# Two more head pairs turned on TensorE, wider weight rows and a re-dealt order of loads and normalising in an attention and feed-forward kernel

## The chip, the cores and the metric

One Trainium2 chip, one of its cores. The metric is the device time of one execution in microseconds (us); lower is better. Three runs of the kernel before gave 489.35, 489.85 and 490.97 us, median 489.85.

## The reference

Attention over 8 batches of 12 heads (448 rows of 64), with one added to the softmax's denominator, then a feed-forward layer with the Mish function over the 3584 rows of 768:

```
scores = matmul(q, k.T) / sqrt(64);  m = max(scores, -1)
e = exp(scores - m)
attn = e / (sum(e, -1) + exp(-m) + 1e-9)
x = matmul(attn, v), heads side by side: [3584, 768]
h = x @ w_in                             # 768 x 2048
out = (h * tanh(softplus(h))) @ w_out    # 2048 x 768
```

Inputs and output are float32; the kernel computes in bfloat16 and sums in float32.

## The kernel before

**Pairs and steps.** Two heads make a pair, 48 pairs in all, numbered here from 0 (the fifth is pair 4, the twelfth pair 11, the sixteenth pair 15). A pair has 7 tiles of 128 query rows against 448 keys, dealt over four steps of 2, 2, 2 and 1 tiles (in the first batches the single tile is the last rows of one head with the first of the other). A step is: TensorE (PE) multiplies the scores into one of three score buffers in PSUM; VectorE (DVE) takes the negated row maximum (`tensor_reduce`, L270); ScalarE (ACT) takes the exponentials into `en` and their sums (L283). `scores_ahead` (L222) keeps the three buffers filled, so the scores of step i+3 come as soon as the exponentials of step i have freed a buffer.

**From exponentials to x.** `denominators` (L295) and `normalise` (L302) scale the 7 tiles of `en` by the reciprocal denominator (L317 on DVE; L315 on GpSimd, which is POOL, for the last pair of a unit). Then `en` is turned so that keys lie on partitions, in tile `eT`. There are two ways. A DMA transposition issued by SyncE (SP) at L321 turns a whole pair. `turn_on_pe` (L326) turns a quarter of a pair (index j) with 7 PE transposes (L332) into a PSUM tile, and a copy of 112x896 elements to `eT` (L336) is put on the list `late`. Pairs in `BY_PE` (5, 6 and 7) go the second way. `av_pair` (L344) multiplies `eT` by v, 8 matmuls at L358, and leaves a copy into `xT` (L367) on `late`. `flush_late` issues what stands on `late`.

**The two mo tiles.** PSUM has two tiles `mo0` and `mo1` outside the score buffers. `mo_take` (L107) hands out the one that was freed first. Turns, q and k transposes, `av_pair` in the first units, and the feed-forward matmuls all take from these two. The order on each engine is the order of the program text. So a PE instruction that takes a tile waits for the copy that last emptied it, and everything behind it on PE waits too.

**Stages.** The head runs the six pairs of batch 0 alone (L511 to L538). Then comes a loop over units u of three pairs (L540). A unit has 12 attention steps n (L551), which also work off a planned list of second matmuls (`mm2_part`, L417) spread by `weight`; then 8 blocks of first matmul and Mish (`mm1_mish`, L375), between which the three pairs are normalised and the next three pairs' q and k are transposed by PE (L179) and copied out. Unit 2 has no second matmuls and no spare work, unit 3 neither; unit 4 (`first_mm2`) is the first that has them, with 5 quarter blocks where later units have 7. Tables place the single acts by unit and step: `TURN_AT` (L491) the quarters turned on PE, `AV_AT` (L496) the av of pairs 3 to 8, `W_AT` (L498) the weight loads.

**Loads.** SP issues q, k and v of a pair, three DMAs of 224 KB (`load_pair`, L114), between its DMA transpositions, all in program order. POOL casts them to bfloat16 (`cast_pair`, L151; pair 0's q and k are cast by DVE and ACT), and issues the weight loads with a cast on the way (`load_w`, L145): 12 pieces of w_in, each [128, 2, 512], three pieces to a quarter of d_ff; and 8 of w_out. The head issues six pieces, units 2, 3 and 4 the rest.

Of the kernel before, what the change touches and what calls it, by code (L numbers as in the profile page):

```python
# [15 lines left out]
UNIT_PAIRS = 3  # L16
# [3 lines left out]
def kernel(  # L20
# [21 lines left out]
    UNITS_PER_B = HP // UNIT_PAIRS  # L42
# [3 lines left out]
    NH = d_model // 2  # L46
# [33 lines left out]
    w_in_sb = singles.tile([128, DM_T, d_ff], BF16)  # L80
# [18 lines left out]
    loaded, casted, qkT, att, xT, gT, o_sbs, stats = {}, {}, {}, {}, {}, {}, {}, {}  # L99
# [3 lines left out]
    def flush_late():  # L103
        while late:
            late.popleft()()
# [5 lines left out]
        return mo_free.popleft()  # L111


    def load_pair(p):  # L114
        if p >= N_PAIRS:
            return
        b, h0 = p // HP, (p % HP) * 2
        tiles = []
        for nm, src in (("q", q), ("k", k), ("v", v)):
            t = ld_pool.tile([SP_, 2, NT * D], FP32, tag=f"{nm}_f", name=f"{nm}_f")  # L120
            nc.sync.dma_start(
                out=t, in_=src[b, h0 : h0 + 2].rearrange("h (p t) d -> p h (t d)", t=NT)
            )
            tiles.append(t)
        loaded[p] = tiles


    def w_pieces():
        c_in, c_out = d_ff // 4, NH
        for i in range(4):  # L130
            for a in range(0, DM_T, 2):
                yield (
                    w_in_sb[:, a : a + 2, i * c_in : (i + 1) * c_in],
                    moe_w_in[a * 128 : (a + 2) * 128, i * c_in : (i + 1) * c_in],
                )
        for h in range(2):
            for f in range(0, FF_T, 4):
                yield (
                    w_out_sb[:, f : f + 4, h * c_out : (h + 1) * c_out],
                    moe_w_out[f * 128 : (f + 4) * 128, h * c_out : (h + 1) * c_out],  # L140
                )
# [6 lines left out]
            nc.gpsimd.dma_start(out=dst, in_=src.rearrange("(a p) c -> p a c", p=128))  # L148


    def cast_pair(p):  # L151
        if p >= N_PAIRS:
            return
        q_f, k_f, v_f = loaded.pop(p)
# [7 lines left out]
        cast_q(out=q_bf, in_=q_f.rearrange(by_t, t=NT))  # L162
        cast_k(out=k_bf, in_=k_f.rearrange(by_t, t=NT))  # L163
        nc.gpsimd.tensor_copy(out=v_bf, in_=v_f)  # L164
        casted[p] = (q_bf, k_bf, v_bf)

    def transpose_pair(p, bank=None):
        if p >= N_PAIRS:
# [53 lines left out]
    def scores_ahead(limit):  # L222

        while rg["next"] < limit and rg["used"] < len(sc_tiles):
            rg["used"] += 1
            scores(rg["next"])
            rg["next"] += 1
# [71 lines left out]
        )  # L299
        nc.vector.reciprocal(out=st["rden"], in_=st["den"])  # L300

    def normalise(p, dma=True, on_pool=False):  # L302
        st = att[p]
        en = st["en"]
        if on_pool:

            st["rden2"] = st_pool.tile([128, NTILE], FP32, tag="rden2", name="rden2")
            nc.vector.tensor_copy(out=st["rden2"], in_=st["rden"])  # L308
        for i in range(NTILE):
            args = dict(  # L310
                out=en[:, :, i, 0:SP_], in0=en[:, :, i, 0:SP_],
                scalar1=st["rden2" if on_pool else "rden"][:, i : i + 1],
            )
            if on_pool:
                nc.gpsimd.tensor_scalar(scalar2=1.0, op0=ALU.mult, op1=ALU.mult, **args)  # L315
            else:
                nc.vector.tensor_scalar(scalar2=None, op0=ALU.mult, **args)  # L317
        eT = eT_pool.tile([128, NT, 2 * S], BF16, tag="eT", name="eT")
        st["eT"] = eT
        if dma:  # L320
            nc.sync.dma_start_transpose(  # L321
                out=eT.rearrange("c j (i q) -> c (j i) q", q=128),
                in_=en.rearrange("q j i c -> q (j i c)"),
            )

    def turn_on_pe(p, j, act=False):  # L326

        st = att[p]
        own = mo_take()
        ps = own[:, :].bitcast(BF16).rearrange("c (i q) -> c i q", q=128)  # L330
        for i in range(NTILE):
            nc.tensor.transpose(ps[0:SP_, i, :], st["en"][:, j, i, 0:SP_], ident)  # L332
        copy = nc.scalar.copy if act else nc.vector.tensor_copy

        def evac():
            copy(  # L336
                out=st["eT"][0:SP_, j, :].rearrange("c (i q) -> c i q", q=128),
                in_=ps[0:SP_, 0:NTILE, :],
            )
            mo_free.append(own)  # L340

        late.append(evac)
# [116 lines left out]
    first_mm2 = 2 * UNITS_PER_B  # L459
# [7 lines left out]
    for g in range(B // 2):  # L467
# [12 lines left out]
        else:  # L480
# [17 lines left out]
    W_AT = ({5: 1, 9: 1}, {1: 1, 4: 1, 5: 1, 7: 1, 9: 1, 11: 1}, {3: 1, 5: 1, 7: 1, 9: 1})  # L498
    for p in range(UNIT_PAIRS):
        load_pair(p)  # L500
    for p in range(2):
        cast_pair(p)
# [36 lines left out]

    for u in range(UNITS_PER_B, N_UNITS + 2 * UNITS_PER_B):  # L540
        attn = u < N_UNITS
# [4 lines left out]
        p0 = u * UNIT_PAIRS  # L546
# [4 lines left out]
        for n in range(steps):  # L551
            pi, s = divmod(n, STEPS)
            p, idx = p0 + pi, p0 * STEPS + n
            late_tp = u == UNITS_PER_B and n == STEPS
            if late_tp:
                transpose_pair(p0 + 2)
            exps(idx)
            if late_tp:
                evac_qk(p0 + 2)
            if u == UNITS_PER_B + 1:  # L560
                for part in TURN_AT[1].get(n, []):
                    turn_on_pe(*part)
            flush_late()
            acc += weight[n]
            want = int(total * acc / sum(weight) + 1e-6)
            while done < want:
                fn, w = filler.popleft()
                fn()
                done += w
            scores_ahead(end)  # L570
            if n in LOAD_AT:
                load_pair(p0 + LOAD_AT.index(n) + LEAD)
                cast_pair(p0 + LOAD_AT.index(n) + LEAD - 1)
            if u - UNITS_PER_B < len(AV_AT):
                early = AV_AT[u - UNITS_PER_B]
                if n in early:
                    av_pair(early[n])
                if u == UNITS_PER_B:
                    for part in TURN_AT[0].get(n, []):
                        turn_on_pe(*part)  # L580
# [65 lines left out]
```

## Time and profile before

| | us |
|---|---|
| median of the runs | 489.85 |
| profiled execution, own time | 492.75 |
| its span | 491.0 |
| PE busy | 450.5 (92%) |
| DVE busy | 351.3 (72%) |
| ACT busy | 350.2 (71%) |
| POOL busy | 161.5 (33%) |

Stretches of the span, read from the timelines and from a table of windows:

| stretch, us | what | PE busy, us | DVE busy, us | ACT busy, us |
|---|---|---|---|---|
| 16 to 30 | head | 7.70 of 14.0 | 13.42 | 12.00 |
| 30 to 47 | head | 10.36 of 17.0 | 14.48 | 15.14 |
| 47 to 66 | end of head, unit 2 attention | 16.78 of 19.0 | 18.06 | 14.08 |
| 66 to 78 | unit 2 first matmul | 11.44 of 12.0 | 9.72 | 7.44 |
| 78 to 94 | unit 3 attention | 11.12 of 16.0 | 14.38 | 14.27 |
| 105.6 to 120.5 | unit 4 attention | 12.90 of 14.9 | 12.02 | 13.61 |
| 132.3 to 149 | unit 5 attention | 14.83 of 16.7 | 10.86 | 13.59 |
| 149 to 162 | unit 5 first matmul | 12.00 of 13.0 | 11.35 | 8.43 |
| 188.6 to 215.3 | a later unit | 26.69 of 26.7 | 21.23 | 21.95 |

How to read the lines that follow: a timeline line is start, duration, engine, source line, operation, what it writes and reads, how often; in brackets stands how long the engine had been idle before it and what ended that. PEld is a weight load on TensorE, SPq is SP's queue. In the strips each digit is a fortieth of the span in tenths busy.

### The profile page before, as it was taken

The page shows a single profiled execution, that of the slowest core. Times are in us where ns is not written, and L with a number is a line of the kernel's source. Part 1 is how long each engine was busy: PE and PEld are TensorE (multiplying, and loading weights), DVE is VectorE, ACT ScalarE, POOL GpSimd, SP SyncE. Part 2 cuts the span into 40 slices and gives each one's busy share as a digit, 9 for nine tenths or more (in the row PEclk, how much of TensorE's full clock was granted, in tenths as well). Part 3 has the DMA queues.
Part 4 walks back from the last instruction along what each step waited for, and adds up shares of the span by engine and source line. Part 5 has one row for each costly group of instructions (what it writes and reads, how often), then busy time and mean ns, then how long its engine had stood idle before and what let it go on. Part 6 is the DMA issues. An engine that isn't in the chain of part 4 may idle for free.

```text
span 491.0 us, 8804 instructions
## 1 busy us (share of the span) xinstructions
PE 450.5 (92%) x2992; PEld 248.5 (51%) x2992; DVE 351.3 (72%) x702; ACT 350.2 (71%) x906; POOL 161.5 (33%) x266
## 2 busy tenths in 40 slices
PE   3556898798989999999999999999999999999996
PEld 1222444454644555555655555555556565556563
DVE  4798987978868787878788786878797878420021
ACT  4889678878777887979796878888797979502300
POOL 3622257454412534253413323253425230300000
PEclk9999998999999999999999999999999999999999
DMA  8999999999999999999998979998999686780112
GB/s 212 183 205 228 236 207 221 228 177 236 175 225 263 195 220 188 241 186 267 148 248 187 223 164 210 211 213 227 176 265 179 167 176 140 132 159 21 45 37 93
DMA packets 209452, 92.19 MB, mean 188 GB/s; under 512 B 166272, under 2 KB 205952, under 8 KB 209408
## 3 DMA queue, kind: packets, MB, share of 16 engines
q1 hardware_dynamic: 201920, 85.35, 81.2%
q0 software_dynamic: 7488, 6.29, 8.8%
q8 instruction: 23, 0.38, 0.3%
q14 instruction: 21, 0.17, 0.1%
HBM read 45.61 MB, written 11.01 MB: 115 GB/s over the span
## 4 chain that ended last, share of the span: by engine, by line
PE 68%; DVE 14%; ACT 9%; DMA 4%; issue 2%; SPq 1%; POOL 0%; DVEq 0%; ACTq 0%
PE mo L446 24%; PE mo L382 23%; PE sc L249 8%; ACT en L283 8%; DVE negm L270 7%; PE sc L358 6%; DVE en L317 4%; PE sc L382 3%; PE sc L179 3%; DMA eT<-en 3%; DMA k_f<-in_k_dram 1%; PE mo L358 1%; PE sc L255 1%; DVE xT L367 1%; DVE eT L336 1%
## 5 line engine op out<-in xcount | busy, mean ns | idle before, releaser
L283 ACT ACTIVATE en<-sc,negm 128x448 bf16<-128x448 f32 x336 | 209.7, 637 | 28.7 <-DVE negm L270 16.3
L270 DVE TENSOR_REDUCE negm<-sc 128x2 f32<-128x896 f32 x192 | 182.4, 969 | 61.5 <-PE sc L249 48.7
L446 PE MATMUL mo<-w_out_sb,gT 128*128 128x384 bf16 (+1 forms) x896 | 142.1, 303 | 0.0
L382 PE MATMUL mo<-xT,w_in_sb 128*128 128x448 bf16 x672 | 140.2, 352 | 0.9 <-DVE xT L367 0.9
L388 ACT ACTIVATE gT<-mo 128x448 bf16<-128x448 f32 x112 | 59.4, 543 | 73.5 <-PE mo L382 73.3
L446 PEld LDWEIGHTS <-gT 128*128 128x128 bf16 x896 | 84.0, 98 | 46.8 <-issue 1.3
L382 PEld LDWEIGHTS <-w_in_sb 128*128 128x128 bf16 x768 | 72.8, 98 | 64.9 <-issue 4.2
L315 POOL TENSOR_SCALAR en<-en,rden 128x448 bf16<-128x448 bf16 x98 | 61.7, 649 | 115.8 <-DVE rden L308 106.0
L249 PE MATMUL sc<-kT,qd 128*128 128x448 bf16 x252 | 71.6, 354 | 1.8 <-DVE qd L210 1.5
L162 POOL CAST q_bf<-q_f 112x512 bf16<-112x512 f32 x47 | 29.1, 619 | 121.8 <-DMA q_f<-in_q_dram 105.4
L283 ACT ACTIVATION_READ_ACCUMULATOR en<-sc,negm 128x1 f32 x336 | 69.2, 206 | 0.0
L317 DVE TENSOR_SCALAR en<-en,rden 128x448 bf16<-128x448 bf16 x238 | 67.2, 354 | 0.9
L433 DVE COPY o_sb<-mo 128x384 f32<-128x384 f32 (+1 forms) x64 | 32.1, 502 | 41.3 <-PE mo L446 41.2
L249 PEld LDWEIGHTS <-qd 128*128 128x128 bf16 x252 | 24.0, 97 | 32.1 <-issue 13.9
L358 PE MATMUL sc<-eT,v_bf 112*64 112x448 bf16 x288 | 34.1, 357 | 4.1 <-ACT en L283 2.0
L164 POOL CAST v_bf<-v_f 112x512 bf16<-112x512 f32 x48 | 29.6, 618 | 20.6 <-DMA v_f<-in_v_dram 19.1
L358 PEld LDWEIGHTS <-v_bf 112*64 112x64 bf16 x384 | 21.1, 114 | 25.7 <-issue 16.9
L255 PE MATMUL sc<-kT,qd 64*128 64x448 bf16 x36 | 17.5, 508 | 17.4 <-ACT en L283 16.0
L163 POOL CAST k_bf<-k_f 112x512 bf16<-112x512 f32 x47 | 29.2, 622 | 6.7 <-DMA k_f<-in_k_dram 5.9
L210 DVE TENSOR_SCALAR qd<-sc 64x448 bf16<-64x448 bf16 x72 | 27.8, 386 | 0.9
L218 ACT COPY kT<-sc 128x448 bf16<-128x448 bf16 x39 | 20.8, 534 | 6.8 <-PE sc L179 6.8
L446 PE MATMUL mo<-w_out_sb,mid 128*128 128x384 bf16 x128 | 24.9, 326 | 0.0
(50 smaller groups left out, 306.9 us busy)
## 6 DMA issues: line engine op xcount, KB each, us to landing
q_f<-in_q_dram SPq DMA_DIRECT2D x48, 224.0 KB, 5.5
k_f<-in_k_dram SPq DMA_DIRECT2D x48, 224.0 KB, 5.6
v_f<-in_v_dram SPq DMA_DIRECT2D x48, 224.0 KB, 5.9
w_in_sb<-in_moe_w_in_dram POOLq DMA_DIRECT2D x12, 256.0 KB, 5.6
w_out_sb<-in_moe_w_out_dram POOLq DMA_DIRECT2D x8, 384.0 KB, 8.6
out_dram<-o_sb SPq DMA_DIRECT2D x7, 336.0 KB, 3.5
out_dram<-o_sb SPq DMA_DIRECT2D x8, 288.0 KB, 4.8
out_dram<-o_sb SPq DMA_DIRECT2D x8, 240.0 KB, 3.4
```

Source lines behind the costliest of these rows:

```text
L163: cast_k(out=k_bf, in_=k_f.rearrange(by_t, t=NT))
L164: nc.gpsimd.tensor_copy(out=v_bf, in_=v_f)
L249: nc.tensor.matmul(sc[:, bk, 0:S], lhsT=qT[:, i].rearrange("d h r -> d (h r)"), rhs=kT, start=True, stop=True,)
L270: nc.vector.tensor_reduce(out=negm, in_=sc[:, 0 : len(cols), 0:S], axis=AX.X, op=ALU.max, negate=True)
L283: nc.scalar.activation(out=st["en"][:, :, c, 0:SP_], in_=sc[:, bk, 0:S].rearrange("q (j c) -> q j c", j=NT), func=AF.Exp, bias=st["negm"][ ...
L315: nc.gpsimd.tensor_scalar(scalar2=1.0, op0=ALU.mult, op1=ALU.mult, **args)
L317: nc.vector.tensor_scalar(scalar2=None, op0=ALU.mult, **args)
L358: nc.tensor.matmul(av[h * 64 : (h + 1) * 64, 0:S], lhsT=v_bf[:, h, j * D : (j + 1) * D], rhs=e_h, start=(j == 0), stop=(j == NT - 1),)
L382: nc.tensor.matmul(h_ps[:, 0:S], lhsT=w_in_sb[:, dm, ff * 128 : (ff + 1) * 128], rhs=xT[b][:, dm, :], start=(dm == 0), stop=(dm == DM_T - 1),)
L388: nc.scalar.activation(out=gT[b][:, ff, :], in_=h_ps[:, 0:S], func=AF.Mish)
L433: nc.vector.tensor_copy(out=o_sb[:, cols], in_=st["o"][:, 0:n_cols])
L446: nc.tensor.matmul(st["o"][:, 0:n_cols], lhsT=src[:, ff, c0 : c0 + 128], rhs=w_out_sb[:, ff, cols], start=(ff == 0), stop=(ff == FF_T - 1),)
```

## The change

Five things. (1) `BY_PE` gains pairs 4 and 11, so these are turned by 4 times 7 PE transposes each and not by DMA; pair 4 in unit 2 at n = 0 to 3, with pair 5 moved from n = 1 to 4 to n = 4 to 7, and pair 11 in unit 4 at n = 2, 4, 5, 7. Two of pair 4's copies go to ACT. In units 2 and 4 a turn now comes before the step's scores, and in unit 2 the av of pairs 3 and 4 come a step later. (2) A w_in piece is [128, 1, 1024]: six pieces to a half of d_ff, 12 in all as before. (3) In the head the 7 tiles of `normalise` are dealt 2, 2, 3 over three steps and no longer all in the second; pair 5's come in unit 2's first three steps. (4) The first three pairs' q and k are loaded ahead of their v, and their v are cast after all q and k. (5) Pair 15 is loaded in unit 4 at n = 0 and no longer in unit 3 at n = 6.

```diff
-    def load_pair(p):
+    def load_pair(p, which="qkv"):
...
-        c_in, c_out = d_ff // 4, NH
-        for i in range(4):
-            for a in range(0, DM_T, 2):
+        c_in, c_out = d_ff // 2, NH
+        for i in range(2):
+            for a in range(DM_T):
                 yield (
-                    w_in_sb[:, a : a + 2, i * c_in : (i + 1) * c_in],
+                    w_in_sb[:, a : a + 1, i * c_in : (i + 1) * c_in],
...
-        for i in range(NTILE):
+        for i in tiles:
...
+        if tiles[-1] < NTILE - 1:
+            return
...
-    BY_PE = (HEAD - 1, HEAD, HEAD + 1)
+    BY_PE = (HEAD - 2, HEAD - 1, HEAD, HEAD + 1, 2 * HEAD - 1)
+    DEALT = ((0, 1), (2, 3), (4, 5, 6))
     TURN_AT = (
-        {1 + j: [(HEAD - 1, j)] for j in range(NT)},
+        {**{j: [(HEAD - 2, j)] for j in range(NT)}, **{4 + j: [(HEAD - 1, j)] for j in range(NT)}},
...
+        {n: [(2 * HEAD - 1, j)] for j, n in enumerate((2, 4, 5, 7))},
     )
-    AV_AT = ({5: 3, 7: 4, 10: 5}, {5: 6, 8: 7, 10: 8})
+    AV_AT = ({6: 3, 8: 4, 10: 5}, {5: 6, 8: 7, 10: 8})
-    for p in range(UNIT_PAIRS):
-        load_pair(p)
+    for which in ("qk", "v"):
+        for p in range(UNIT_PAIRS):
+            load_pair(p, which)
...
-    cast_pair(2)
+    cast_pair(2, with_v=False)
+    for p in range(UNIT_PAIRS):
+        cast_v(p)
...
-            if s == 1:
-                if p:
-                    normalise(p - 1)
+            if s < len(DEALT) and p:
+                normalise(p - 1, dma=p - 1 not in BY_PE, tiles=DEALT[s])
...
-    normalise(HEAD - 1, dma=HEAD - 1 not in BY_PE)
+
+    def turn_parts(u, n):
+        for p, j in TURN_AT[u - UNITS_PER_B].get(n, []):
+            turn_on_pe(p, j, act=p == HEAD - 2 and j % 2 == 1)
...
             flush_late()
+            if u == UNITS_PER_B:
+                turn_parts(u, n)
...
+            if u == first_mm2:
+                turn_parts(u, n)
             scores_ahead(end)
+            if u == UNITS_PER_B and n < len(DEALT):
+                normalise(HEAD - 1, dma=False, tiles=DEALT[n])
             if n in LOAD_AT:
-                load_pair(p0 + LOAD_AT.index(n) + LEAD)
-                cast_pair(p0 + LOAD_AT.index(n) + LEAD - 1)
+                i = LOAD_AT.index(n)
+                if u == first_mm2 and i == 0:
+                    load_pair(p0 + LEAD - 1)
+                if u != first_mm2 - 1 or i < 2:
+                    load_pair(p0 + i + LEAD)
+                cast_pair(p0 + i + LEAD - 1)
...
-                if u == UNITS_PER_B:
-                    for part in TURN_AT[0].get(n, []):
-                        turn_on_pe(*part)
```

More of the change, by code (lines that the diff above doesn't have):

```diff
@@ L117, in load_pair @@
         b, h0 = p // HP, (p % HP) * 2
-        tiles = []
+        tiles = loaded.setdefault(p, [])
         for nm, src in (("q", q), ("k", k), ("v", v)):
+            if nm not in which:
+                continue
             t = ld_pool.tile([SP_, 2, NT * D], FP32, tag=f"{nm}_f", name=f"{nm}_f")
@@ L124, in load_pair @@
             tiles.append(t)
-        loaded[p] = tiles
     def w_pieces():
-        c_in, c_out = d_ff // 4, NH
-        for i in range(4):
-            for a in range(0, DM_T, 2):
+        c_in, c_out = d_ff // 2, NH
+        for i in range(2):
+            for a in range(DM_T):
                 yield (
-                    w_in_sb[:, a : a + 2, i * c_in : (i + 1) * c_in],
-                    moe_w_in[a * 128 : (a + 2) * 128, i * c_in : (i + 1) * c_in],
+                    w_in_sb[:, a : a + 1, i * c_in : (i + 1) * c_in],
+                    moe_w_in[a * 128 : (a + 1) * 128, i * c_in : (i + 1) * c_in],
                 )
@@ L148, in load_w, with cast_v, cast_pair @@
             nc.gpsimd.dma_start(out=dst, in_=src.rearrange("(a p) c -> p a c", p=128))
-    def cast_pair(p):
+    def cast_v(p):
+        nc.gpsimd.tensor_copy(out=casted[p][2], in_=loaded.pop(p)[2])
+    def cast_pair(p, with_v=True):
         if p >= N_PAIRS:
             return
-        q_f, k_f, v_f = loaded.pop(p)
+        q_f, k_f = loaded[p][:2]
         q_bf = bf_pool.tile([SP_, NT, 2, D], BF16, tag="q_bf", name="q_bf")
@@ L163, in cast_pair @@
         cast_k(out=k_bf, in_=k_f.rearrange(by_t, t=NT))
-        nc.gpsimd.tensor_copy(out=v_bf, in_=v_f)
         casted[p] = (q_bf, k_bf, v_bf)
+        if with_v:
+            cast_v(p)
     def transpose_pair(p, bank=None):
@@ L300, in denominators, with normalise @@
         nc.vector.reciprocal(out=st["rden"], in_=st["den"])
-    def normalise(p, dma=True, on_pool=False):
+    def normalise(p, dma=True, on_pool=False, tiles=range(NTILE)):
         st = att[p]
@@ L507 @@
     load_pair(3)
-    cast_pair(2)
+    cast_pair(2, with_v=False)
+    for p in range(UNIT_PAIRS):
+        cast_v(p)
     for p in range(HEAD):
@@ L560 @@
             if u == UNITS_PER_B + 1:
-                for part in TURN_AT[1].get(n, []):
-                    turn_on_pe(*part)
+                turn_parts(u, n)
             flush_late()
+            if u == UNITS_PER_B:
+                turn_parts(u, n)
             acc += weight[n]
@@ L569 @@
                 done += w
+            if u == first_mm2:
+                turn_parts(u, n)
             scores_ahead(end)
+            if u == UNITS_PER_B and n < len(DEALT):
+                normalise(HEAD - 1, dma=False, tiles=DEALT[n])
             if n in LOAD_AT:
[L572 to L573 removed]
+                i = LOAD_AT.index(n)
[4 more added lines that the diff above has]
+                cast_pair(p0 + i + LEAD - 1)
             if u - UNITS_PER_B < len(AV_AT):
@@ L577 @@
                     av_pair(early[n])
-                if u == UNITS_PER_B:
-                    for part in TURN_AT[0].get(n, []):
-                        turn_on_pe(*part)
             elif s == (2 if pi else 0) and N_PAIRS <= p < N_PAIRS + UNIT_PAIRS:
```

2 lines of the change are left out of this document (1 added, 1 removed).

## The prediction

> **What bounds the kernel now.** I read the page's strips first, then the timelines of PE, DVE, POOL and SP's queue up to 165 us, then the chain that ended last.
>
> ```profile
> PE   3556898798989999999999999999999999999996
> DVE  4798987978868787878788786878797878420021
> ```
>
> From the fourteenth slice (160 us) on PE is full; a later unit has 26.69 us of PE work in 26.7. Nothing in the change touches those units, so all is decided before 162 us, by when PE work begins and by how much is added. Before that PE is idle for 40.5 us of the span (491.0 less 450.5), most of it in the head, where DVE sets the pace (13.42 busy of 14.0 in 16 to 30 us).
>
> ```profile
> 10.57 0.62 POOL L162 CAST q_bf<-q_f 112x512 bf16<-112x512 f32 x1 [0.36 <-DMA q_f<-in_q_dram]
> 11.55 0.62 POOL L163 CAST k_bf<-k_f 112x512 bf16<-112x512 f32 x1 [0.36 <-DMA k_f<-in_k_dram]
> 41.25 0.80 POOL L162 CAST q_bf<-q_f 112x512 bf16<-112x512 f32 x1 [5.64 <-PE sc L258]
> ```
>
> Casts of pairs 2 and 7. At the start loads land 0.97 us apart and each cast waits for its own. The third line is released, I think, by its load (issued at 35.44, next view), since the engine named was long done.
>
> ```profile
> 22.73 5.65 SPq L321 DMA_TRANSPOSE eT<-en  x1
> 28.48 0.53 SPq L121 DMA_DIRECT2D q_f<-in_q_dram  x1
> ...
> 30.10 5.25 SPq L321 DMA_TRANSPOSE eT<-en  x1
> 35.44 0.53 SPq L121 DMA_DIRECT2D q_f<-in_q_dram  x1
> ```
>
> SP is a second chain: a transposition holds its queue for over 5 us, and the loads of pairs 6 and 7 stand behind.
>
> ```profile
> 57.14 0.53 PE L179 MATMUL mo<-ident,q_bf 112*128 112x112 bf16 x4 [0.41 <-DVE eT L336]
> ...
> 58.82 0.91 PE L332 MATMUL mo<-ident,en 128*112 128x128 bf16 x7 [0.27 <-DVE kT L216]
> ```
>
> In unit 2, PE work that takes an mo tile waits for the DVE copy that empties it.
>
> ```profile
> 125.13 12.44 DMA eT<-en
> 137.57 0.04 issue
> 137.61 0.95 PE sc L358 x8
> ```
>
> In the chain, pair 12's transposition takes 12.44 us (median of the transpositions 7 to 8), while four w_out loads run, and PE idles 1.87 us before 137.61.
>
> **Part by part.**
>
> *q and k ahead of v.* Pair 1's q and k move up one slot (0.97 us), pair 2's two (1.95). By the row of casts, pair 2's k is cast at 9.6 and not 11.55. Pair 3 still lands at 13.49 to 14.5, so its transposes keep the gain of the steps to some 1.5 us. The v casts move behind; no av needs v before 35 us, so nothing is paid.
>
> *Normalising dealt.* DVE's work is the same. It fills the 0.25 us that DVE waits in each pair after the denominators, about 1 us over the head. But the DMA transposition now follows one reduce (1.0) later. For pair 0: 22.73 less 1.5, plus 1.0, less 0.25: about 22.0. So the SP chain gains 0.7. Pairs 6 and 7 are loaded behind it, and PE's transposes of pair 7 and the av behind them give the last scores of the head's fifth pair (44.79). DVE, ahead by 1.75 by then, waits there. I take 0.7 of gain at 47 us; the bounds are 0 (the SP chain unmoved) and 2.5 (1.5 and 1.0, SP not binding).
>
> *Pair 4 by PE.* Removed: one SP transposition (about 6 us of the queue, after 51 us), so the loads of pairs 9 to 11, issued at 57.31 to 65, start up to 6 us earlier. That matters in one place: pair 8's normalise at 67.87 took 3.34 us beside POOL's casts of these loads; alone 7 tiles took 1.80. PE's wait for the q that comes behind it (0.56 us at 71.56) goes: 0.56 gained. Added in unit 2: 28 transposes on PE, four times 0.95 us as 58.82 shows; two copies on DVE (0.55 each, 1.1); two on ACT, not in the trace in this shape: between 0.53 (a 448-wide copy) and 1.1 (two of them), I take 0.8; ACT has 4.9 us idle in 47 to 66 to hide them. DVE is full from 46 to 61.4, so 1.1 counts. Then the order: at n = 4 the chain is now pair 8's transposes, DVE's two copies, pair 5's first turn in the tile so freed, and only then the scores. DVE has no work for 1.0 us (turn 0.55 and scores 0.36 at the faster rows, 0.95 and 0.55 at the slower: 1.5). At the end pair 4's and 5's avs and the last copy of pair 5 stand one behind another. Stepping the rows through n = 0 to 11: the last but two of the large reduces ends at 62.3 against 61.4, the first matmul begins at 67.6 against 65.89, the head's 0.7 included: **+1.7**. Least is +0.3 (1.1 of copies less 0.7 and 0.1 of DVE idle time), most +4.0 (all PE rows slow to the end).
>
> Which rows PE runs at is a term of its own. The same 8 av matmuls take 1.7 us up to 64 us and 0.95 later; 7 transposes 0.99 or 0.55. At 82 to 85.6 the profile gives a granted clock of 0.55 beside the slow rows; before 65 us it gives 1.00 beside equally slow ones, so there I go by durations. PE became fast at 64.8, after its first 3 us without a gap, and again at 85.5, after 3.3. I use slow rows to n = 6. The Trainium skill (TensorE: Matmul & The Clock Gate, "Part 1: The HAM clock gate") says a busy window of about 3.4 us releases the clock and that windows run freely; the two stretches here agree. By that rule the denser PE work could be fast from about 54 us, and unit 2 would come to +1.3 by the fast rows above.
>
> *w_in in wider rows.* Same 12 issues, 0.72 us each on POOL; half the packets. Landing took 4.3 to 9.4 us. All six of the second half are needed at the start of unit 3's matmuls (93.84), not the last three at 99.7: the twelfth is issued at 85.66 and lands 7.6 later, 93.3, and its matmul is the sixth, at 94.8. Cover 1.5 us; gone, a late piece would cost its lateness. DMA saved between 0 and half of a piece's time; off the path: 0.
>
> *Pair 11 by PE.* Removed: the third transposition of SP before 112.86, so loads start at about 108. Added in unit 4: 28 transposes, 4 times 0.55 = 2.2 us, where PE has 2.0 idle, and four DVE copies (2.2) where DVE has 2.9. That would nearly fit. But each turn takes an mo tile whose copy is only issued in the next step, and second matmuls hold the other tile.
>
> ```profile
> 115.21 0.62 DVE L270 TENSOR_REDUCE negm<-sc 128x1 f32<-128x448 f32 x1 [0.78 <-PE sc L249]
> 115.75 0.61 DVE L367 CAST xT<-sc 128x448 bf16<-128x448 f32 x1
> 116.29 2.08 DVE L270 TENSOR_REDUCE negm<-sc 128x2 f32<-128x896 f32 x2
> ```
>
> At n = 5 the turn needs the tile of n = 4's turn, whose copy stands on DVE behind the small reduce, now at 115.8 (0.6 later by n = 4's turn ahead of the av): reduce to 116.4, copy to 116.95, turn to 117.55, scores to 117.95, and the next reduce starts at 118.0, not 116.29. At n = 7 the tile is that of the second-matmul block just ended: reduce to 120.55, its copy to 121.0, turn, scores, next reduce at 122.05, not 118.75. At n = 8 the av waits for the last copy at 123.6. The exponentials end 3.5 us later, the first matmul begins at about 124.8, 4.2 later than 120.54. PE so reaches pair 12's av at 135.74 + 4.2 = 139.9. The transposition starts 3.5 later, but the w_out loads start about 1.7 earlier, so it lands at about 137.6 and PE's 1.87 is gone: 139.9 against 137.61, +2.3. ACT, which idled 2.44 at 140.23 for the same wait, has caught up, and of the 1.0 that PE waits for q at 155.46 I take 0.7 off: **+1.6**. Bounds: -1.3 (everything fits, exponentials 0.5 late, av -1.0, q -0.3) and +3.
>
> *Sixteenth load later.* Three DMAs (2.9 us at 0.97) leave a DMA-full stretch in unit 3 and join unit 4's, where SP is free 5 us earlier. POOL's cast of pair 15 now waits there, to some 114; behind it stand the casts of 16 and 17 and four w_out loads, needed after 122. Hidden: 0.
>
> **Sum:** +1.7 - 0.56 + 1.6 = +2.7 on a span of 491.0 (492.75 with what lies around it). The profiled execution is 2.9 above the median; the difference carries over: 489.85 + 2.7, some **492.5**.
>
> **Rivals.** A difference under 0.3% (1.5 us: 488.4 to 491.3) can't be told from none.
> - *The turns fit.* If DVE's copies come in time for the tiles, unit 2 costs +0.3 and unit 4 with 5 gives -1.3: with -0.56, -1.6, 488.3. For it: DVE's 2.9 idle in unit 4; unit 3 turns eight quarters in an attention part hardly longer than unit 4's. Against: the waits at 57.14 and 58.82. One of two fits: 489.9 to 491.2.
> - *The head keeps its gain.* If SP's chain doesn't bind, 1.8 more: 486.5 where the turns fit, 490.7 where not. For it: DVE is the fuller engine at 16 to 30. Against: the cast at 41.25.
> - *PE stays slow through unit 2*: 2.3 more, 494.8. It decides if no 3 us without a gap come before n = 10. Against: PE is denser than before.
> - By the clock rule above 0.4 less, 492.1: within the forecast.
>
> **Chances.** Forecast 0.45 (its own range 491.3 to 494.5); turns fit 0.15 (0.10 of it beyond 0.3%); one fits 0.15; head keeps its gain, with the turns fitting, 0.17; PE slow 0.08. Faster 0.10 + 0.17 = 0.27; same 0.05 + 0.15 = 0.20; slower 0.53. The range 487.0 to 495.0 takes in all but about half of the fourth case and the tail above the fifth.
>
> **What would show it.** Right: pair 2's k cast near 9.6; SP's first transposition near 22; DVE idle about 1 us at unit 2's n = 4; PE waits before L332 in unit 4 released by DVE L336 and L433; no wait on eT in unit 5; the granted clock as before. Wrong: unit 4's exponentials within 1 us of 14.9 us, or the head's end more than 1.5 us earlier.

## The result and the profile after

| | before | after |
|---|---|---|
| median, us | 489.60 (4 runs) | 496.07 (4 runs) |
| ratio, 95% interval | | 1.0135 (1.0103 to 1.0167) |
| profiled execution, own time | 492.75 | 496.93 |
| its span | 491.0 | 495.1 |
| PE busy | 450.5 | 453.1 |

The change makes the kernel 6.5 us slower by the medians (6.6 by the ratio). The forecast was 2.7 us slower, and 496.07 lies above its range.

The strips of the changed kernel's page:

```profile
PE   4565688897999999999999999999999999999996
PEclk9999698899899999999999999999999999999999
DVE  4886876987678786888878786878697877520021
```

PE's first digit is 4 and not 3: the head's steps come earlier from the second pair on. But the fifth (49.5 to 61.9 us, the start of unit 2) is 6 and not 8, the sixth 8 and not 9, and the tenth (unit 4's attention) 7 and not 8. The granted clock is down in the fifth slice and in the eleventh (124 to 136), where it was 9 before.

POOL's timeline of the changed kernel, pair 2's q and k and then pair 7's q:

```profile
8.46 0.61 POOL L166 CAST q_bf<-q_f 112x512 bf16<-112x512 f32 x1 [0.73 <-DMA q_f<-in_q_dram]
9.43 0.61 POOL L167 CAST k_bf<-k_f 112x512 bf16<-112x512 f32 x1 [0.35 <-DMA k_f<-in_k_dram]
...
41.81 0.61 POOL L166 CAST q_bf<-q_f 112x512 bf16<-112x512 f32 x1 [7.18 <-DMA q_f<-in_q_dram]
```

Pair 2's q and k are cast 2.1 us earlier (k at 9.43 and not 11.55), and by pair 7 nothing is left: 41.81 against 41.25. SP's queue in the changed kernel shows where it went:

```profile
22.00 5.93 SPq L328 DMA_TRANSPOSE eT<-en  x1
27.98 0.56 SPq L123 DMA_DIRECT2D q_f<-in_q_dram  x1
...
29.65 5.59 SPq L328 DMA_TRANSPOSE eT<-en  x1
35.33 0.53 SPq L123 DMA_DIRECT2D q_f<-in_q_dram  x1
35.96 1.50 SPq L123 DMA_DIRECT2D k_f<-in_k_dram  x1
```

The first transposition begins 0.73 us earlier, the second 0.45 and the load of pair 7's q only 0.11, because both transpositions hold the queue some 0.3 longer. From that issue to the cast of q it is then 6.5 us, where it was 5.8 before. PE reaches pair 7's transposes early and waits for them, first in the changed kernel, then in the kernel before:

```profile
42.48 0.56 PE L184 MATMUL mo<-ident,q_bf 112*128 112x112 bf16 x4 [3.89 <-POOL q_bf L166]
```

```profile
42.11 0.55 PE L179 MATMUL mo<-ident,q_bf 112*128 112x112 bf16 x4 [0.29 <-POOL q_bf L162]
```

PE's waits of 43 to 132 us, summed by what was waited for, in the changed kernel (columns: who <- whom: sum, times, longest):

```profile
PE mo L339 <- DVE eT L343: 3.4, 4, 1.4
...
PE mo L339 <- DVE o_sb L440: 1.6, 2, 1.1
PE mo L339 <- DVE en L322: 1.2, 2, 0.9
...
PE mo L184 <- DVE eT L343: 1.1, 1, 1.1
PE mo L339 <- DVE kT L221: 0.8, 1, 0.8
PE mo L453 <- DVE eT L343: 0.8, 1, 0.8
...
PE mo L365 <- DVE eT L343: 0.6, 1, 0.6
```

L339 is the turn, L343 the copy that empties a turned quarter's tile. Waits for such copies are the largest group, 5.9 us: by turns (3.4), by pair 8's transposes (L184, 1.1), by a second matmul (L453, 0.8) and by an av (L365, 0.6). The same view of the kernel before lists 0.4 by those transposes and 0.3 by an av. Two places of PE's timeline, unit 2 and unit 4 of the changed kernel:

```profile
53.85 0.91 PE L339 MATMUL mo<-ident,en 128*112 128x128 bf16 x7 [1.43 <-DVE eT L343]
54.69 0.55 PE L260 MATMUL sc<-kT,qd 64*128 64x448 bf16 x1
...
57.77 0.53 PE L184 MATMUL mo<-ident,q_bf 112*128 112x112 bf16 x4 [1.11 <-DVE eT L343]
...
59.45 0.90 PE L339 MATMUL mo<-ident,en 128*112 128x128 bf16 x7 [0.78 <-DVE kT L221]
60.28 0.58 PE L268 MATMUL sc<-kT,qd 64*64 64x448 bf16 x1
...
65.59 0.55 PE L339 MATMUL mo<-ident,en 128*112 128x128 bf16 x7 [0.58 <-DVE eT L343]
...
120.20 0.55 PE L339 MATMUL mo<-ident,en 128*112 128x128 bf16 x7 [0.99 <-DVE eT L343]
120.59 0.54 PE L254 MATMUL sc<-kT,qd 128*128 128x448 bf16 x2
...
124.37 0.82 PE L339 MATMUL mo<-ident,en 128*112 128x128 bf16 x7 [1.14 <-DVE o_sb L440]
```

Scores (`sc`) stand right behind the turn that waits. DVE in turn has nothing to reduce until they are there:

```profile
53.18 0.62 DVE L343 COPY eT<-mo 112x896 bf16<-112x896 bf16 x1
53.72 1.08 DVE L275 TENSOR_REDUCE negm<-sc 128x2 f32<-128x896 f32 x1
...
60.98 0.62 DVE L275 TENSOR_REDUCE negm<-sc 128x1 f32<-128x448 f32 x1 [1.58 <-PE sc L271]
```

The PE wait that ends at 53.85 is the pattern in small: the tile's copy runs at 53.18, after the step's reduces and normalising, though its turn was over by 51.3.

In the chain that ended last, unit 5 of the changed kernel has no transposition in it; second matmuls run through to pair 12's av:

```profile
140.65 3.27 PE mo L453 x28
143.92 0.88 PE sc L365 x8
```

Stage starts on PE, from the profiled executions, us. The last row is the attention part of unit 4 alone. Pair 5 is the sixth and last pair of the head; the prediction calls it the fifth.

| | before | after | differs by | forecast |
|---|---|---|---|---|
| last scores of the head's pair 5 (`64*64`) | 44.79 | 45.16 | +0.4 | -0.7 |
| first matmul of unit 2 | 65.89 | 69.28 | +3.4 | +1.7 |
| second matmul of unit 4 | 105.64 | 108.60 | +3.0 | +1.1 |
| first matmul of unit 4 | 120.54 | 129.08 | +8.5 | +5.3 |
| second matmul of unit 6 | 161.94 | 167.00 | +5.1 | +2.7 |
| unit 4, second to first matmul | 14.90 | 20.48 | +5.6 | +4.2 |

### The profile page after: what moved, and what is told of

Read it like the earlier page. It is cut to its first block, busy times and chain, and to the rows that moved or that the text cites. A ratio compares the mean times of both kernels' runs of the same rounds, so it can differ in the third digit from the quotient of the medians.

```text
span 495.1 us, 8920 instructions
## 1 busy us (share of the span) xinstructions
PE 453.1 (92%) x3048; PEld 253.9 (51%) x3048; DVE 349.1 (71%) x708; ACT 352.6 (71%) x908; POOL 159.2 (32%) x266
## 3 DMA queue, kind: packets, MB, share of 16 engines
q0 software_dynamic: 5952, 6.29, 8.8%
## 4 chain that ended last, share of the span: by engine, by line
PE 80%; DVE 9%; ACT 6%; DMA 2%; issue 2%; SPq 0%; POOL 0%; DVEq 0%; POOLq 0%
PE mo L453 27%; PE mo L389 26%; PE sc L254 9%; PE sc L365 6%; DVE negm L275 6%; ACT en L288 5%; PE sc L389 4%; PE sc L184 3%; PE mo L339 2%; DVE en L322 1%; DMA q_f<-in_q_dram 1%; PE mo L365 1%; DVE eT L343 1%; PE sc L260 1%; DMA k_f<-in_k_dram 1%
## 5 line engine op out<-in xcount | busy, mean ns | idle before, releaser
L453 PE MATMUL mo<-w_out_sb,gT 128*128 128x384 bf16 (+1 forms) x896 | 142.6, 304 | 0.8 <-DVE eT L343 0.8
L453 PEld LDWEIGHTS <-gT 128*128 128x128 bf16 x896 | 84.4, 98 | 48.0 <-issue 2.7
L322 DVE TENSOR_SCALAR en<-en,rden 128x448 bf16<-128x448 bf16 x238 | 64.0, 336 | 1.1
L440 DVE COPY o_sb<-mo 128x384 f32<-128x384 f32 (+1 forms) x64 | 32.1, 501 | 41.4 <-PE mo L453 41.3
L365 PE MATMUL sc<-eT,v_bf 112*64 112x448 bf16 x288 | 34.6, 361 | 0.6 <-ACT en L288 0.4
L365 PEld LDWEIGHTS <-v_bf 112*64 112x64 bf16 x384 | 20.4, 112 | 21.5 <-issue 14.2
L453 PE MATMUL mo<-w_out_sb,mid 128*128 128x384 bf16 x128 | 24.9, 326 | 0.0
L184 PEld LDWEIGHTS <-q_bf 112*128 112x128 bf16 x192 | 14.4, 103 | 20.1 <-POOL q_bf L166 6.4
```

What stands on the lines that cost most here:

```text
L184: nc.tensor.transpose(by_s[s][:, t * SP_ : (t + 1) * SP_], src[:, t].rearrange("p h d -> p (h d)"), ident[:SP_, :SP_],)
L365: nc.tensor.matmul(av[h * 64 : (h + 1) * 64, 0:S], lhsT=v_bf[:, h, j * D : (j + 1) * D], rhs=e_h, start=(j == 0), stop=(j == NT - 1),)
L440: nc.vector.tensor_copy(out=o_sb[:, cols], in_=st["o"][:, 0:n_cols])
L453: nc.tensor.matmul(st["o"][:, 0:n_cols], lhsT=src[:, ff, c0 : c0 + 128], rhs=w_out_sb[:, ff, cols], start=(ff == 0), stop=(ff == FF_T - 1),)
```

## The experiments

Each run is set beside runs of the kernel before on the same chip (17 to 35 of them, medians 488.87 to 490.04), and its ratio is to those. "+x" is the ratio less one, times 489.6.

**First theory:** the loss is the turns' (pair 11 in unit 4, pair 4 in unit 2). **Rival:** the re-dealt order around them costs by itself. The first three take turns out of the changed kernel; the fourth puts pair 11's alone into the kernel before.

*Without pair 11's turns:*

```diff
-    BY_PE = (HEAD - 2, HEAD - 1, HEAD, HEAD + 1, 2 * HEAD - 1)
+    BY_PE = (HEAD - 2, HEAD - 1, HEAD, HEAD + 1)
-        {n: [(2 * HEAD - 1, j)] for j, n in enumerate((2, 4, 5, 7))},
+        {},
```

> The changed kernel with pair 11 turned by DMA again, all else kept. Tile theory (turns wait for an mo tile and the copy that empties it): unit 4's attention part shrinks from 20.5 us (108.6 to 129.1) to about 15 as before, but the wait for pair 12's transposition (1.9 us) and for q (1.0) come back; some 2 to 3 us less than the changed kernel's 496.1, so 493 to 494. Rival A (the loss is made before 66 us, in the head and unit 2, and unit 4's stretch is only idle time that would come later anyway): less than 1 us off, 495 to 496.5.

Measured 496.12, ratio 1.0120 (1.0086 to 1.0153): no better. Unit 4's attention part is back at 14.90, but two waits on PE have come in its place, in this run's timeline:

```profile
129.74 0.55 PE L254 MATMUL sc<-kT,qd 128*128 128x448 bf16 x2 [1.87 <-DVE qd L215]
141.92 0.95 PE L365 MATMUL sc<-eT,v_bf 112*64 112x448 bf16 x8 [2.27 <-DMA eT<-en]
```

The first is pair 15's q: its load, moved to unit 4, now stands behind three DMA transpositions. So "sixteenth load later costs nothing" holds only because pair 11's transposition has left SP's queue.

*Without pair 4's turns* (pair 4 out of `BY_PE` and out of `TURN_AT[0]`):

> The changed kernel with pair 4 turned by DMA again; pair 5's turns stay at n = 4 to 7. Tile theory: unit 2's first matmul starts some 2 to 3 us earlier than at 69.3; the wait of 0.6 us for the q behind pair 8's normalising may return; 493.5 to 494.5. Rival B (the head's SP queue is what costs, since it brings pair 7 late): pair 4's transposition is behind pair 7's load, so the head is as late as before, and with one transposition more in SP's queue nothing is won: 496 or more.

Measured 494.12, ratio 1.0080 (1.0053 to 1.0106). Taking pair 4's turns out wins back 2.7 us by the ratios, 2.0 by the medians.

*Without either:*

> The changed kernel with pairs 4 and 11 both by DMA: what is left is wider w_in rows, dealt normalising, q and k ahead of v, pair 15's load later. If the two turns make the whole loss and add up: 490 to 491.5, the time of the kernel before plus the 0.4 us that the head is late. If the head's parts cost by themselves: 493 or more. If the rest is a gain that the turns hid: 488 or less.

Measured 494.28, ratio 1.0086 (1.0052 to 1.0120). If the turns were all of the loss this had to be near 490. It isn't: 4.2 us are still lost, and the wait for pair 15's q, here again with 1.88 us on PE, is less than half of that. The first theory falls as far as unit 2 goes.

*The kernel before with pair 11's turns alone:*

```diff
-    BY_PE = (HEAD - 1, HEAD, HEAD + 1)
+    BY_PE = (HEAD - 1, HEAD, HEAD + 1, 2 * HEAD - 1)
...
+        {n: [(2 * HEAD - 1, j)] for j, n in enumerate((2, 4, 5, 7))},
...
+            if u == first_mm2:
+                for part in TURN_AT[2].get(n, []):
+                    turn_on_pe(*part)
             scores_ahead(end)
```

> The kernel before with pair 11 alone turned by PE in unit 4 at n = 2, 4, 5, 7 ahead of the step's scores. Tile theory: unit 4's attention part grows by 4 to 5.5 us, 3 of it given back in unit 5, so 491.5 to 493 against 489.6. Rival A: 489 to 490.5, within what can be told from none.

Measured 492.58, ratio 1.0053 (1.0030 to 1.0076): +2.6 from this alone.

**Second theory:** pair 11's loss isn't the turning, but that each copy is issued in the step after its turn. *The same with the turn ahead of the flush,* so that its copy goes out in the same step:

```diff
+            if u == first_mm2:
+                for part in TURN_AT[2].get(n, []):
+                    turn_on_pe(*part)
             flush_late()
...
-            if u == first_mm2:
-                for part in TURN_AT[2].get(n, []):
-                    turn_on_pe(*part)
             scores_ahead(end)
```

> As the kernel before with pair 11 alone by PE (492.6), but the turn stands ahead of the step's issue of waiting copies, so that its copy goes to DVE in the same step, ahead of the next reduce. The same 28 transposes and four copies. Tile theory: PE no longer stands before the turns at n = 5 and 7; unit 4's attention part takes 15.5 to 17 us and not 19.6, and as the later waits stay away the time is 488 to 490.5, at or below the kernel before. Rival (28 transposes and four copies are simply too much work for unit 4): 18.5 us or more there and 491.5 or more.

Measured 489.32, ratio 0.9989 (0.9975 to 1.0004): the +2.6 are gone. The sums of PE's waits from 103 to 124 us, first of the run with late copies, then of this one:

```profile
PE mo L332 <- DVE o_sb L433: 1.6, 2, 1.1
PE mo L332 <- DVE eT L336: 1.4, 2, 1.0
PE mo L446 <- DVE eT L336: 0.8, 1, 0.8
PE sc L358 <- DVE eT L336: 0.6, 1, 0.6
```

```profile
PE mo L446 <- DVE o_sb L433: 1.7, 1, 1.7
PE mo L332 <- DVE o_sb L433: 0.8, 1, 0.8
```

2.8 us of waits for `eT` copies have gone, and unit 4's attention part falls from 19.6 to 17.2. What stays is the wait for the second matmuls' copies (`o_sb`). One thing is not separated here: in unit 4 the edit also puts the turn ahead of the step's second matmuls on PE, where it stood behind them. So of the +2.6, the part of the copy's place and the part of the turn's place are known only together.

*Single parts in the kernel before.* The dealt normalising of the head's pairs 0 to 4:

```diff
-            if s == 1:
-                if p:
-                    normalise(p - 1)
+            if s < len(DEALT) and p:
+                normalise(p - 1, dma=p - 1 not in BY_PE, tiles=DEALT[s])
```

> The kernel before with only the head's normalising of pairs 0 to 4 dealt 2, 2, 3 over three steps; pair 5's whole as before. Theory of SP's queue: the DMA transpositions start a reduce (1 us) later, the loads of pairs 6 and 7 behind them come as much later, and the head's scores before unit 2 start 0.5 to 1.5 us later: 490 to 491.5. Rival (DVE's idle 0.25 us in each pair is won): 488.5 to 489.3.

Measured 490.39, ratio 1.0015 (1.0001 to 1.0029): no gain, and at most a small loss, +0.7. Next, q and k of the first three pairs ahead of their v (that part of the change's diff):

> The kernel before with only the first three pairs' q and k ahead of their v. If SP's queue sets the head: its first transposition starts 1.5 us earlier with the steps, and nothing holds it back: a gain of 0.7 to 1.5 us, 488.2 to 489. If the loads of pairs 6 and 7 are bound by what the DMA engines still have to move: 489.3 to 490, no gain.

Measured 490.35, ratio 1.0006 (0.9980 to 1.0032): no gain either. Next, unit 2's order (pair 5 dealt over n = 0 to 2, turned at 4 to 7 ahead of the scores, the avs of pairs 3 and 4 a step later, pair 4 still by DMA):

> The kernel before with only unit 2 rearranged as in the changed kernel, pair 4 still by DMA: pair 5 normalised in n = 0 to 2, turned at n = 4 to 7 ahead of the scores, av of pairs 3 and 4 a step later. If the moved order by itself makes the 1.5 to 2 us that the changed kernel without pair 4 still loses between the head's last scores and unit 2's first matmul: 491 to 492. If it comes from what stands in SP's and POOL's queues there: 489 to 490.

Measured 490.07, ratio 0.9999 (0.9975 to 1.0024): nothing. Then the wider rows alone, and the changed kernel with the old rows:

> The kernel before with only w_in in rows of 1024. By the prediction it costs and gains nothing: 489.3 to 490.7. Rival (a piece of one block of rows is dealt over the DMA engines in another way and lands late, or slows the loads beside it, so that the head's loads of pairs 6 and 7 come later): 491 to 493, with the head's last scores later by 1 us or more.

> The changed kernel with w_in in rows of 512 again, all else kept. If the rows cost: 494.5 or less against 496.1. If they don't: 495.5 to 496.7.

Measured 488.51, ratio 0.9990 (0.9969 to 1.0011), and 496.04, ratio 1.0139 (1.0113 to 1.0164): the rows do nothing that can be told from none, though queue q0 went from 7488 packets to 5952.

*The dealing and unit 2's order together, in the kernel before:*

> The kernel before with the dealt normalising of all six head pairs and unit 2's order together, pair 4 by DMA. Each alone came to 490.1 to 490.4. If they add up: 490 to 491. If the two together are what the changed kernel without either turn still loses (494.3): 492 or more, with unit 2's first matmul 2 us later than in the kernel before, because the av of pairs 4 and 5 come behind the last scores.

Measured 491.41, ratio 1.0043 (1.0024 to 1.0062): +2.1, between the two expectations.

*The changed kernel with pair 11's turns ahead of the flush:*

```diff
-            if u == UNITS_PER_B + 1:
+            if u in (UNITS_PER_B + 1, first_mm2):
                 turn_parts(u, n)
             flush_late()
...
-            if u == first_mm2:
-                turn_parts(u, n)
```

> The changed kernel with pair 11's turn ahead of the step's issue of waiting copies, as in the earlier run. Tile theory: unit 4's attention part comes from 20.5 to about 17.2 us and 3 us go, of which little comes back later since the waits in unit 5 are already away: 493 to 494. Rival (in the changed kernel the time is set elsewhere): 495.5 or more.

Measured 493.92, ratio 1.0089 (1.0060 to 1.0118): some 2.2 less. That left about 4.4 in the head and unit 2.

**Third theory and its rival** for these 4.4: the avs' later place, or the dealing. The changed kernel with `AV_AT` as before; the run of dealing and order with it as before; the changed kernel with the head's normalising in one piece:

```diff
-    AV_AT = ({6: 3, 8: 4, 10: 5}, {5: 6, 8: 7, 10: 8})
+    AV_AT = ({5: 3, 7: 4, 10: 5}, {5: 6, 8: 7, 10: 8})
```

> The changed kernel with unit 2's av of pairs 3 and 4 back at n = 5 and 7 (as before), all else of the change kept. Theory 'avs behind the last scores': the last two avs no longer stand one behind another after the last scores (3.2 us of PE in the profiled runs with the new order against 1.2 with the old), so unit 2's first matmul comes about 2 us earlier, and the median falls from about 496.1 to 494. Rival 'the dealing': the reduces of the head are late, not the avs, and the avs' place changes less than 0.5: 495.6 to 496.5.

> The kernel before with the dealt normalising (all six pairs) and pair 5's turns at n = 4 to 7 ahead of the scores, but the avs of pairs 3 and 4 at n = 5 and 7 as before. The run with the avs a step later took 2.5 more than before (1.0043). If the avs' place is the cause, this one takes 0 to 0.5 more than before; if the dealing is, it stays at 2 to 2.5 more.

```diff
-            if s < len(DEALT) and p:
-                normalise(p - 1, dma=p - 1 not in BY_PE, tiles=DEALT[s])
+            if s == 1 and p:
+                normalise(p - 1, dma=p - 1 not in BY_PE)
```

> The changed kernel with the head's normalising of pairs 0 to 4 back in one piece in the second step (pair 5's still dealt in unit 2). Theory 'dealing': the DMA transpositions start about 1 us earlier and the exponentials are not held up, so unit 2 begins about 1.5 to 2.5 earlier and the median is 493.5 to 494.5. Rival 'avs': no change beyond 0.5, 495.6 to 496.5.

Measured, in this order: 496.40, ratio 1.0135 (1.0116 to 1.0154); 490.77, ratio 1.0030 (1.0007 to 1.0054); 495.25, ratio 1.0125 (1.0105 to 1.0145). In the changed kernel neither gives back more than 0.5 us of the 4.4, so theory and rival both fall as its cause. The middle run came out between its two expectations (+1.5) and decides nothing.

*The parts that cost nothing, together* (kernel before, pair 11 copied at once, wider rows, sixteenth load later):

> The kernel before with the three parts that cost nothing or gained: pair 11 turned by PE with its turn ahead of the flush (so that it is copied out in the same step), w_in in rows of 1024, pair 15 loaded in unit 4. Pair 11's turns alone in this way gave 0.9989 of before. If the sixteenth load in unit 3 collides with anything there, this gains up to 1 more: ratio 0.997; if it is covered, the ratio is that of the turn alone, 0.9975 to 1.0004, which can't be told from none.

Measured 489.09, ratio 0.9993 (0.9977 to 1.0009): no gain that can be told from none.

**Fourth theory:** unit 2 loses by the same late copies as unit 4. Unit 2 has no second matmuls, so there this edit leaves PE's order as it is and moves the copies alone. *The changed kernel with the turns of both units ahead of the flush:*

```diff
-            if u == UNITS_PER_B + 1:
+            if u - UNITS_PER_B < len(TURN_AT):
                 turn_parts(u, n)
             flush_late()
-            if u == UNITS_PER_B:
-                turn_parts(u, n)
...
-            if u == first_mm2:
-                turn_parts(u, n)
```

> The changed kernel with the turns of units 2 and 4 ahead of the flush, so that every turn is copied out in its own step and not in the next. In unit 4 alone this gave 493.9 where the changed kernel took 496.1. Theory 'late copies everywhere': unit 2's waits for tiles (1.43, 1.11, 0.58 and 0.60 us in the changed kernel's trace, all released by copies of turns) go in the same way, and the median is 491.5 to 492.5. Rival 'DVE is full in unit 2': the copies then delay the reduces by as much as PE gains, and it stays at 493.5 to 494.5.

Measured 490.00, ratio 1.0007 (0.9984 to 1.0031). It took away more than the theory had said: nearly the whole loss. PE's waits from 43 to 132 us in this run, the three largest (the changed kernel's are shown above):

```profile
PE sc L268 <- ACT en L288: 2.7, 2, 2.1
PE sc L260 <- ACT en L288: 2.7, 5, 0.9
PE mo L453 <- DVE o_sb L440: 1.7, 1, 1.7
```

No turn waits for a turn's copy any more; the scores wait for ACT, as in the kernel before. On DVE the copy now runs in the step of its turn, ahead of the next reduce (the turn ended at 50.7):

```profile
51.51 0.59 DVE L343 COPY eT<-mo 112x896 bf16<-112x896 bf16 x1
52.01 0.61 DVE L275 TENSOR_REDUCE negm<-sc 128x1 f32<-128x448 f32 x1
```

and on PE turns and scores of unit 2 follow each other here with no gap but one for ACT:

```profile
51.14 0.99 PE L339 MATMUL mo<-ident,en 128*112 128x128 bf16 x7
52.06 0.55 PE L260 MATMUL sc<-kT,qd 64*128 64x448 bf16 x1
52.06 0.55 PE L263 MATMUL sc<-kT,qd 64*128 64x448 bf16 x1
52.55 0.99 PE L339 MATMUL mo<-ident,en 128*112 128x128 bf16 x7
54.37 0.53 PE L260 MATMUL sc<-kT,qd 64*128 64x448 bf16 x1 [0.82 <-ACT en L288]
```

From the head's last scores to unit 2's first matmul it is 21.7 us, against 24.1 in the changed kernel and 21.1 before. The other profiled runs bear this out: 24.0 to 25.7 in all six that turn pair 4 on PE with late copies in unit 2, 20.1 to 21.1 in all seven with the old order. The run that has only unit 4's copies at once took 25.7, so that unit 2's alone are worth 4.0 there.

*The same with the head's normalising in one piece:*

> The same with the head's normalising of pairs 0 to 4 back in one piece in the second step. The changed kernel without the dealing took 495.25 (0.8 less, intervals touching). If the two effects add up, 0.5 to 1 below the run beside it: 491 on the first theory, 493 on the rival. If the dealing has no effect of its own, the same as the run beside it.

Measured 489.47, ratio 1.0003 (0.9984 to 1.0022): beside the run with it, the dealing has no effect of its own that these runs can tell.

The ledger, all of it on the changed kernel:

| version | ratio | loss, us |
|---|---|---|
| as it is | 1.0135 | 6.6 |
| unit 4's copies at once | 1.0089 | 4.4 |
| unit 2's and 4's at once | 1.0007 | 0.3 |

So some 4.0 us (1.0089 less 1.0007; by the two intervals 2.2 to 5.8) are late copies in unit 2 and some 2.2 the late place of turn and copy in unit 4 (in the kernel before it was 3.1, 1.0053 less 0.9989). With all copies at once the 56 added transposes cost nothing that can be measured, and nor does anything else in the change gain. No version beat the kernel before by more than its measurement tells; the nearest is pair 11 copied at once, 0.9989.

## Why the prediction was wrong in size

The direction was right and so was the mechanism in unit 4: a turn ahead of the scores takes a tile whose copy is only issued a step later. The step that failed is unit 2's part of the sum, which counted only one of the same waits there. What was off, the largest first:

1. **Unit 2's +1.7.** The step said "then the order: at n = 4" and named this one wait and the avs at the end; n = 1 to 3 and the turns behind n = 4 were taken to fit. DVE does idle at n = 4 (1.58 us at 60.98, forecast 1.0 to 1.5), but the rule that the prediction spelled out for unit 4 ("a copy only issued in the next step") holds in unit 2 as well: 53.85, 57.77 and 65.59 are waits of it. Before, a turn stood behind the step's scores, and its wait did not hold them; ahead of them it delays the scores, then DVE, then ACT. The prediction costed the position for unit 4 and not for unit 2. The late copies measured about 4.0 (the last two lines of the ledger). The forecast had 1.4 for them: 1.7, less the 0.3 that it gave for the case in which the turns fit.
2. **The head's 0.7 of gain.** Pair 2's k was cast at 9.43 (forecast 9.6) and SP's first transposition began at 22.00 (forecast 22.0), yet the head's last scores came at 45.16 and not 44.1. The step took SP's 0.7 through to the end of the chain; the queue gave it back within two transpositions (22.00, 29.65, then the load of pair 7 at 35.33 against 35.44). That SP's queue binds was right: PE stands 3.89 us at 42.48 for that load. Two traces alone don't settle the size, since the head's end scatters: 43.35 to 45.48 in eight profiled runs with both changes to the head, 42.83 to 44.79 in six with the old one. They show no gain; the lower bound, 0, is nearest.
3. **Unit 4's 4.2.** The waits came where they were forecast: at n = 5 (120.20, released by L343) and n = 7 (124.37, released by L440). Their size was 5.6 in the changed kernel and in three more runs with the same turns (20.44 to 20.49 for the attention part) and 4.7 in two others (19.65 without pair 4's turns, 19.64 with pair 11's alone). The 0.8 between is PE's clock, which fell in the four and not in the two. These are rows of the windows table of the changed kernel (columns: stretch, length, PE busy, granted clock, share of DMA, GB/s), and the turn at n = 7 in the run without pair 4's turns:

```profile
120.00:124.00 4.00, 2.28 (x17) 1.00 1.16 241
124.00:128.00 4.00, 3.63 (x23) 0.57 1.31 203
128.00:132.00 4.00, 4.00 (x35) 1.00 1.06 163
```

```profile
122.65 0.55 PE L339 MATMUL mo<-ident,en 128*112 128x128 bf16 x7 [1.14 <-DVE o_sb L440]
```

   Beside the 0.57 an av took 1.46 us and seven transposes 0.82, against 0.95 and 0.55 elsewhere in the unit. In the other run the stretch that lies as far ahead of its turn (118.28 to 122.28) has the same busy time, 2.28 of 4, and its granted clock stayed at 1.00. So the same work led to the drop in four runs and not in two; in the five runs with unit 4's copies at once it did not come.
4. **"The difference carries over."** The profiled execution of before was 2.9 us above its median and that of after only 0.9, so the traces differ by 4.1 in span and the medians by 6.5. In the trace of before unit 2's first matmul began at 65.89; in six other profiled runs with the same order of unit 2 it began at 63.5 to 64.7. The forecast was worked out from an execution that was late there, as though the change kept that excess.

In the terms of the sum, 2.7 were forecast and 6.6 measured (by the ratio). Of the 3.9 between, the late copies of unit 2 make 2.6 (4.0 against 1.4). Those of unit 4 came out at 2.2 against 2.9 (its 1.6, less the -1.3 that the prediction gives when everything fits), 0.7 the other way. The rest is what the change does with all copies at once: 0.3 slower (by its interval 0.8 faster to 1.5 slower) against 1.6 faster, 1.9 off; the three make up the 3.9 but for rounding. The forecast's 1.6 rests on its credits: the head's 0.7, the 0.56 of the q wait and the 1.3 of units 4 and 5. Which of them failed to reach the end is shown only in part, by the head above and unit 5 below.

What held in the traces: the q wait of 0.56 at 71.56 is gone; unit 5 has no wait on `eT`; two ACT copies took 0.90 each (taken as 0.8, between 0.53 and 1.1); rows of 1024 and the sixteenth load cost nothing, the latter only because pair 11's transposition is gone, as its step said. Of the 1.87 us that PE waited for `eT` in unit 5 the forecast took credit for all; two of the other executions with pair 11 by DMA (the dealt head and the rows alone) don't have that wait, so a part of that credit wasn't there to be had. Of the prediction's own signs one failed: the granted clock was not as before, but down in units 2 and 4.

The rivals: that the turns fit would have been nearly right had the copies gone out at once (0.3 slower rather than 1.6 faster). That the head keeps its gain is refuted by the cast at 41.81 and PE's wait for it.

On PE's clock the prediction misread its own lines. It has PE become fast at 64.8 in the kernel before, "after its first 3 us without a gap"; but from 52.00 to 56.70 PE was busy 4.70 of 4.70 us there and its scores stayed at 0.55 to 0.58. The granted clock reads 1.00 beside these slow rows, so the durations decide. In the changed kernel scores were fast early (0.36 us at 47.10) and slow again from 54.69 (0.55) to 61.72, where the forecast had slow rows up to n = 6. The Trainium skill (TensorE: Matmul & The Clock Gate, "Part 1: The HAM clock gate") lets a busy window of 3.4 us release the clock and an idle one take it back. By that rule, the prediction said, PE could be fast from about 54, a gain of 0.4 beside the forecast. The changed kernel's trace agrees with the release: PE ran without a gap from 42.48 to 46.17 and from 59.45 to 63.1, and its rows were fast from 47.10 and from 63.13. It doesn't agree with the taking back: the turn at 53.85 is slow again, and since 47.10 PE had no gap longer than 1.43 us.

What the forecast hoped for did not come because the turns waited: from 53.85 to 59.45 PE's longest stretch without a gap is 2.8 us, and from 52 to 58 and from 58 to 64 us the granted clock is 0.57 and 0.58, with PE busy 3.46 and 4.71 us of 6.

Left open: unit 2's order alone cost nothing in the kernel before (0.9999) and with the dealt head +2.1 (1.0043). The intervals allow that the two simply add up, and no run shows a mechanism for more. Late copies of pair 5's turns are not seen to be it: in the profile of the two together PE waits 0.4 us for such a copy in unit 2 and 0.7 for the copy of pair 8's k.

## What to carry to other kernels

When work that takes one of two recycled tiles is moved ahead of the work that feeds the pacing engine, issue the copy that frees the tile in the same step; moving the turns ahead of the flush was worth 6.3 us of 6.6 here. Having found such a wait in one stage, go through every other stage with the same order and cost it there too. And a gain at the start of a chain that runs through a queue is nothing until it is seen at the chain's end, nor is one profiled execution the median: ask how far it lies from it, and where.

## What the runs showed of the hardware

- PE's granted clock fell in unit 4 in four of the six profiled runs with late copies there. In the changed kernel the four microseconds from the turn at n = 7 on (124.37) read 0.57, 0.50, 0.50 and 0.73, which is some 3.4 us at 0.50 (an estimate from these figures). In the 2 us ahead PE was busy 0.33, with no gap over 1.14. In the other two runs the same records stood ahead of that turn and the clock stayed at 1.00.
- The granted clock can read 1.00 beside rows at half speed: in the kernel before from 52.00 to 56.70 us, with scores of 0.55 us that take 0.36 at 71.56.
- An issue of a load on SP's queue, 0.40 to 0.56 us elsewhere between 22 and 38 us, took 1.50 once (35.96).
- Half the w_in packets (queue q0: 5952 where there were 7488, the same 6.29 MB) took the same share of the DMA engines' time, 8.8%, in the pages of the kernel before and the changed kernel.
